# One run of twelve matmuls for a head's value product, in place of six steps

## The chip, the cores and the metric

The kernel runs on one NeuronCore of a Trainium2 chip. The metric is the device time of one execution in microseconds (us), the median of several runs. TensorE (PE) does matmuls, and its weight loads are shown apart as PEld. VectorE is DVE, ScalarE is ACT, GpSimd is POOL, and SyncE (SP) issues the DMAs. Each engine has its own instruction stream. Where one needs another's result, it waits on a semaphore.

## The reference

Two layers follow each other. Attention comes first, with 4 batches, 8 heads, a sequence of 768 and a head size of 64. Keys outside a query's hash bucket are masked out.

```python
mask = q_bucket[:, :, :, None] == k_bucket[:, :, None, :]
scores = np.where(mask, scale * np.matmul(q, k.transpose(0, 1, 3, 2)), -1000000000.0)
attn = np.exp(scores - np.max(scores, axis=-1, keepdims=True))
attn = attn / (np.sum(attn, axis=-1, keepdims=True) + 1e-09)
attn_out = np.matmul(attn, v)
```

Then, with x of [4, 768, 512] put together from the 8 heads, a gated feed-forward layer with a causal convolution of width 5:

```python
gate = 1 / (1 + np.exp(-sum(conv_w[k] * xp[:, k:k + S, :] for k in range(5))))
out = (gate * (x @ w_val)) @ w_out
```

All is float32 (the feed-forward weights are float64 and are turned into float32 pairs in the kernel).

## The kernel before, in words

A unit is one head of one batch (32 units). A unit has six tiles of 128 queries, so there are 192 tiles. The main loop has one **slot** k per tile, 196 in all, and the order in which the loop's body issues instructions is the order in which each engine takes them (a manual schedule). Nothing reorders them later.

In slot k the loop issues, for each engine:

- ACT: two copies `pt` of the transposed weights of tile k-4 out of PSUM (`keep_transposed`), then the exponential `p` of tile k.
- DVE: the row maximum `nm` of tile k, the factor `gs`, the shift `nb` (and, in even slots, row sums and reciprocals of two tiles), then what the side work asks for.
- POOL: the normalising of tile k-2, and subtractions of the side work.
- PE: the scores `s` of tile k+1 (four matmuls, tiles `ak`,`aq` and `bk`,`bq`), then the side work's matmuls, then six transposes `tp` of tile k-3.

The scores have two PSUM buffers, so the scores of tile k+2 can be issued only when the exponential of tile k has read its buffer. The transposes have two buffers `tp`. The value product has one, `av`, and the feed-forward sums have one, `m`, while the loop runs.

The side work is cut into steps by Python generators. A list holds the generators of one kind, and `step` advances the first of them to its next `yield`:

- `avs` (`attn_v`): the value product of a unit. It is entered at the sixth tile's copy, which is in slot k with k % 6 == 3. Six steps, one for each block of 128 keys, two matmuls each (two halves of 384 queries, placed in the two column halves of the array). After the last step, ACT copies the result into `x`.
- `convs` (`pair_x`): for two heads together, the split of `x` in two parts (`xh` on DVE, `xl` on POOL), an empty step, five convolution steps of 768 columns on DVE, and after a batch's fourth pair the sigmoids on ACT.
- `moes` (`moe`): the feed-forward of a batch. A value chunk (`val`, called V below) has three steps of four matmuls. After the third, DVE multiplies with the gate (`ht`), and at the next step's end casts the product (`hh`), from which POOL subtracts (`hl`). An output chunk (`outp`, called O below) has three steps of four matmuls with 512 columns and then a copy out of PSUM, on ACT or, near the sigmoids, on DVE. The last two output chunks of a batch are held back until the next batch's feed-forward has been entered.
- `weights`: loading and converting the feed-forward weights, on all engines but PE.
- `preps`: a unit's operands (cast `aq` on DVE in a slot with k % 6 == 5, subtraction `bq` on POOL and DMAs in the next), and every fourth unit the hash bits (`u` on DVE after 8 small matmuls).

After the loop come what is left of `avs`, the last convolutions and sigmoids, and the last batch's feed-forward.

## Time and profile before

| | |
|---|---|
| median of 3 runs | 646.72 us (646.63 to 647.21) |
| the profiled execution, its span from first to last instruction | 645.6 us |
| what lies outside of the span, against the median | 1.1 us |
| PE busy | 610.7 us, 95% of the span |
| DVE busy | 489.4 us, 76% |
| ACT busy | 424.5 us, 66% |
| POOL busy | 355.5 us, 55% |
| granted TensorE clock | 0.991 mean |

The span counts from the first to the last instruction of one profiled execution. Shares are averages over stages which differ: weights are converted in the first quarter, the feed-forward works beside the attention later, and it is alone at the end. A matmul in float32 is two PE instructions. In rows of the timeline the first number is the start in us from the span's start, and the second is the time from the start of the first to the end of the last instruction merged into the row. PE's instructions overlap, so what one costs is the distance between starts.

### The profile page before, as it was taken

What the parts mean: (1) busy time and instruction counts of PE and PEld (TensorE: products, weight loads), DVE (VectorE), ACT (ScalarE), POOL (GpSimd) and SP (SyncE); (2) the same over time, 40 slices, a digit from 0 to 9 for tenths busy, and PEclk for the clock granted to TensorE, in tenths of its full rate; (3) what the DMA queues carried; (4) which work ended last, traced back from release to release, by engine and by line L of the source; (5) the groups of instructions that cost most, each with busy time, mean ns of one, the idle gap of its engine ahead of it and who ended that gap; (6) DMA issues with size and microseconds to landing.
All of it is one profiled execution on the core that took longest, in us unless ns stands there. A gap on an engine that the chain in (4) does not pass through costs nothing.

```text
span 645.6 us, 10637 instructions
## 1 busy us (share of the span) xinstructions
PE 610.7 (95%) x3496; PEld 412.7 (64%) x3496; DVE 489.4 (76%) x1064; ACT 424.5 (66%) x881; POOL 355.5 (55%) x326
## 2 busy tenths in 40 slices
PE   4799998988999999999999999999999999999997
PEld 2565554555557666676667776676657777666895
DVE  5788999999996876769785887658695787656532
ACT  3487776767778666667878676576788666665300
POOL 1375868577765663566653656456563566536221
PEclk9799999999999999999999999999999999999999
DMA  6533435343432324233333234243332313300111
GB/s 239 126 100 78 137 102 136 110 123 89 104 78 66 81 66 133 70 103 95 103 79 104 59 79 118 71 117 79 99 75 60 79 30 79 84 18 1 49 50 49
DMA packets 23269, 56.76 MB, mean 88 GB/s; under 512 B 4296, under 2 KB 4296, under 8 KB 23216
## 3 DMA queue, kind: packets, MB, share of 16 engines
q1 hardware_dynamic: 23072, 56.06, 32.2%
q8 instruction: 28, 0.46, 0.3%
q14 instruction: 25, 0.20, 0.1%
q10 hardware_dynamic: 144, 0.03, 0.0%
HBM read 23.12 MB, written 6.29 MB: 46 GB/s over the span
## 4 chain that ended last, share of the span: by engine, by line
PE 70%; DVE 20%; ACT 5%; DMA 2%; issue 2%; POOL 0%; SPq 0%; DVEq 0%; ACTq 0%
PE av L303 17%; PE s L232 16%; PE tp L280 16%; PE m L390 8%; PE m L365 7%; DVE nm L238 7%; DVE nb L248 3%; ACT p L256 2%; DVE g L334 2%; DVE w L100 1%; PE tp L365 1%; PE tp L390 1%; PE s L390 1%; DVE gs L244 1%; PE tp L194 1%
## 5 line engine op out<-in xcount | busy, mean ns | idle before, releaser
L271 POOL TENSOR_SCALAR p<-p,ri 128x768 f32<-128x768 f32 x192 | 211.8, 1108 | 212.6 <-DVE nb L248 142.6
L289 ACT COPY pt<-tp 128x384 f32<-128x384 f32 x384 | 165.2, 481 | 100.9 <-PE tp L280 99.4
L256 ACT ACTIVATE p<-s,nb,gs 128x768 f32<-128x768 f32 x192 | 191.9, 1000 | 56.4 <-DVE nb L248 51.4
L238 DVE TENSOR_REDUCE nm<-s 128x1 f32<-128x768 f32 x192 | 182.5, 951 | 48.3 <-PE s L232 47.7
L280 PEld LDWEIGHTS tp<-ident,p 128*128 128x128 f32 x1152 | 125.4, 142 | 112.5 <-issue 75.4
L280 PE MATMUL tp<-ident,p 128*128 128x128 f32 x1152 | 169.4, 284 | 0.8 <-ACT pt L289 0.4
L303 PE MATMUL av<-pt,vt 128*64 128x384 f32 x768 | 168.7, 511 | 0.3 <-ACT x L311 0.3
L232 PE MATMUL s<-ak,aq 76*128 76x384 f32 x384 | 118.0, 388 | 24.9 <-ACT p L256 20.3
L232 PE MATMUL s<-bk,bq 128*128 128x384 f32 x384 | 102.2, 348 | 0.0
L232 PEld LDWEIGHTS s<-ak,aq 76*128 76x128 f32 x384 | 59.5, 195 | 36.9 <-ACT p L256 29.2
L303 PEld LDWEIGHTS av<-pt,vt 128*64 128x64 f32 x768 | 41.3, 135 | 58.8 <-issue 51.3
L248 DVE TENSOR_TENSOR nb<-nm,gs 128x1 f32<-128x1 f32 x192 | 73.8, 384 | 3.6 <-DVE ri L266 0.2
L334 DVE SCALAR_TENSOR_TENSOR g<-x,cw_sb,g 128x768 f32<-128x768 f32 x64 | 72.9, 1139 | 0.2
L232 PEld LDWEIGHTS s<-bk,bq 128*128 128x128 f32 x384 | 72.0, 194 | 0.4 <-issue 0.4
L168 POOL TENSOR_TENSOR bq<-r,aq 128x768 fp32r<-128x768 f32 x31 | 58.3, 1882 | 0.5 <-DVE aq L166 0.5
L376 POOL TENSOR_TENSOR hl<-ht,hh 128x384 fp32r<-128x384 f32 x32 | 32.8, 1026 | 32.3 <-DVE hh L374 32.3
L324 POOL TENSOR_TENSOR xl<-x,xh 128x384 fp32r<-128x384 f32 x32 | 33.2, 1050 | 29.6 <-DVE xh L323 29.6
L365 PE MATMUL m<-xh,wv 128*128 128x384 f32 x200 | 42.6, 337 | 0.0
L311 ACT COPY x<-av 64x384 f32<-64x384 f32 x64 | 30.3, 473 | 17.9 <-PE av L303 17.0
L370 DVE TENSOR_TENSOR ht<-m,g 128x384 f32<-128x384 f32 x25 | 13.9, 557 | 32.8 <-PE m L365 29.1
L256 ACT ACTIVATION_READ_ACCUMULATOR p<-s,nb,gs 128x1 f32 x192 | 38.6, 201 | 0.0
L390 PE MATMUL m<-wo,hh 128*128 128x512 f32 x144 | 38.2, 395 | 0.0
(84 smaller groups left out, 471.5 us busy)
## 6 DMA issues: line engine op xcount, KB each, us to landing
r<-in_qk_dram SPq DMA_DIRECT2D x32, 384.0 KB
vt<-in_v_dram SPq DMA_DIRECT2D x16, 384.0 KB
out_dram<-o SPq DMA_DIRECT2D x24, 256.0 KB
ak<-aq SPq DMA_DIRECT2D x31, 192.0 KB
bk<-aq SPq DMA_DIRECT2D x31, 192.0 KB
bk<-bq SPq DMA_DIRECT2D x31, 192.0 KB
bq<-aq SPq DMA_DIRECT2D x31, 192.0 KB
w<-in_w_val_dram SPq DMA_DIRECT2D x4, 512.0 KB
```

What stands on the lines that cost most here:

```text
L168: nc.gpsimd.tensor_tensor(out=bq, in0=r, in1=aq.bitcast(FP32), op=ALU.subtract)
L232: nc.tensor.matmul(out=s[:, hf, 0:HS], lhsT=lq[0:n, qs], rhs=rk[0:n, hf * HS:(hf + 1) * HS], start=n == M, stop=n == P)
L238: nc.vector.tensor_reduce(out=nm, in_=s[:, :, 0:HS], axis=AX.XY, op=ALU.max, negate=True)
L248: nc.vector.tensor_tensor(out=nbs[k], in0=nms.pop(k), in1=gs[k], op=ALU.mult)
L256: nc.scalar.activation(out=p, in_=s[:, :, 0:HS], func=AF.Exp, bias=nb, scale=gs.pop(k), accum_out=sm[:, k % 2:k % 2 + 1])
L271: nc.gpsimd.tensor_scalar(out=p, in0=p, scalar1=rcs.pop(k), scalar2=1.0, op0=ALU.mult, op1=ALU.mult)
L280: nc.tensor.transpose(out=tp[:, n * P:(n + 1) * P], in_=p[:, kb * P:(kb + 1) * P], identity=ident)
L289: nc.scalar.copy(out=pt[:, :, qo:qo + P], in_=tp[:, 0:HS].rearrange("p (a b) -> p a b", b=P))
L303: nc.tensor.matmul(out=av[s * D:(s + 1) * D, 0:HS], lhsT=vt[:, kb, hh * D:(hh + 1) * D], rhs=pt[kb // 3][:, kb % 3, :], start=(kb == 0), s ...
L334: nc.vector.scalar_tensor_tensor(out=g, in0=x[:, k:k + S], scalar=w, in1=g, op0=ALU.mult, op1=ALU.add)
L365: nc.tensor.matmul(out=acc[:, 0:HS], lhsT=wv[wi][:, c, j * P:(j + 1) * P], rhs=xs_[(c, o)][xi], start=(m == 0), stop=(m == 11))
L390: nc.tensor.matmul(out=acc, lhsT=hs[(o, j)][hi][:, tb * P:(tb + 1) * P], rhs=wo[wi][:, j, :], start=(m == 0), stop=(m == 11))
```

## The change

In the slot in which a unit's value product is entered (k % 6 == 3), all six steps are now done, one run of 12 matmuls and the copies into `x`. That slot does no feed-forward step and up to four convolution steps. Of the other five slots, odd ones do a convolution step (all of them after a batch's last pair, and in the last ten slots) and each does one feed-forward step, the one with k % 6 == 1 two. Slots after the sigmoids still do three. Comments have been taken out as well.

```diff
@@ attn_v
         if hh == 1:
             if c == 0:
                 cur["xs"], cur["g"] = {}, []
+            cur["last"] = c == NP - 1
             convs.append(pair_x(b, c, x, cur["g"], cur["xs"]))
...
-    cur["gates"], cur["end"], cur["pts"] = 0, False, []
+    cur["gates"], cur["end"], cur["pts"], cur["last"] = 0, False, [], False
...
             if k < N:
                 exponentials(k)
-            if k >= 60 or k % 2:
+            whole = bool(avs)
+            for _ in range(4 if whole else 1 if k % 2 or k >= N - 10 or cur["last"] else 0):
                 step(convs)
             for _ in range((1, 0, 2, 0, 2, 2)[k % 6]):
                 step(weights[turn])
                 turn = 1 - turn
-            for _ in range(3 if cur["gates"] else 1):
+            for _ in range(0 if whole else 3 if cur["gates"] else 1 + (k % 6 == 1)):
                 step(moes)
             cur["gates"] = max(0, cur["gates"] - 1)
             step(preps)
-            step(avs)
+            finish(avs)
             if 0 <= k - LAG < N:
                 transposes(k - LAG)
```

What this makes of the order is shown for slots 117 to 121, a stretch with six value steps to a unit. First PE in slots 117 and 118, before:

```order
L232 MATMUL s<-ak,aq 128x384 x2
L232 MATMUL s<-bk,bq 128x384 x2
L365 MATMUL m<-xh,wv_118 128x384 x4
L303 MATMUL av<-pt,vt 64x384 x2
L280 MATMUL tp<-ident,p 128x128 x6
L232 MATMUL s<-ak,aq 128x384 x2
L232 MATMUL s<-bk,bq 128x384 x2
L365 MATMUL m<-xh,wv_119 128x384 x4
L303 MATMUL av<-pt,vt 64x384 x2
L280 MATMUL tp<-ident,p 128x128 x6
```

PE in the same two slots, now (117 is a slot with k % 6 == 3):

```order
L232 MATMUL s<-ak,aq 128x384 x2
L232 MATMUL s<-bk,bq 128x384 x2
L303 MATMUL av<-pt,vt 64x384 x12
L280 MATMUL tp<-ident,p 128x128 x6
L232 MATMUL s<-ak,aq 128x384 x2
L232 MATMUL s<-bk,bq 128x384 x2
L366 MATMUL m<-xl,wv_118 128x384 x4
L280 MATMUL tp<-ident,p 128x128 x6
```

All twelve `av` matmuls stand in slot 117 between the scores of tile 118 and the transposes of tile 114, the value step of that slot is gone, and slot 118 has no `av`. The chunk of value steps ends in 118 (its third group is the one with `xl`).

PE in slot 121, now:

```order
L232 MATMUL s<-ak,aq 128x384 x2
L232 MATMUL s<-bk,bq 128x384 x2
L366 MATMUL m<-xl,wv_118 128x384 x4
L366 MATMUL m<-xh,wv_118 128x384 x4
L280 MATMUL tp<-ident,p 128x128 x6
```

The slot with two feed-forward steps ends one chunk and begins the next, in the one buffer `m`.

DVE in slots 118 to 120 (after the four convolution steps of slot 117), now:

```order
L238 TENSOR_REDUCE nm<-s 128x1
L262 TENSOR_SCALAR s_4550<-sm 128x2
L244 TENSOR_SCALAR gs<-nm 128x1
L266 RECIPROCAL ri<-s_4550 128x2
L248 TENSOR_TENSOR nb<-nm,gs 128x1
L371 TENSOR_TENSOR ht<-m,g 128x384
L238 TENSOR_REDUCE nm<-s 128x1
L244 TENSOR_SCALAR gs<-nm 128x1
L248 TENSOR_TENSOR nb<-nm,gs 128x1
L335 SCALAR_TENSOR_TENSOR g<-x,cw_sb,g 128x768
L375 CAST hh<-ht 128x384
L166 CAST aq<-r 128x768
```

The product `ht` stands in slot 118 ahead of the maximum of tile 119, and a convolution step, `hh` and `aq` stand in slot 119 ahead of the maximum of tile 120. Before, the products stood in other slots (119 and 122 among them), beside convolution steps of single slots.

## The prediction

> **What bounds the kernel now.** I read busy time by stages first. The first row runs from the scores of tile 10 (just ahead of the first value step) to those of tile 58, the second from there to the end of the last value product. Columns: length; PE, PEld, DVE, ACT, POOL busy with their instructions; PE's clock; DMA.

> ```profile
> 38.09:174.42 136.33, 121.70 (x705) 72.04 (x705) 129.54 (x269) 99.52 (x214) 93.37 (x82) 1.00 0.40 109
> 174.42:599.38 424.96, 423.23 (x2492) 287.47 (x2489) 314.37 (x707) 301.13 (x625) 237.93 (x219) 1.00 0.30 78
> ```

> DVE sets the pace of the first stretch (129.5 of 136.3 us), PE of the second (423.2 of 425.0). The tail to 645.6 takes 46.3 us. The groups of costs on DVE (mean ns behind the comma):

> ```profile
> L248 DVE TENSOR_TENSOR nb<-nm,gs 128x1 f32<-128x1 f32 x192 | 73.8, 384 | 3.6 <-DVE ri L266 0.2
> L334 DVE SCALAR_TENSOR_TENSOR g<-x,cw_sb,g 128x768 f32<-128x768 f32 x64 | 72.9, 1139 | 0.2
> L166 DVE CAST aq<-r 128x768 fp32r<-128x768 f32 x31 | 18.5, 596 | 0.0
> L323 DVE CAST xh<-x 128x384 fp32r<-128x384 f32 x32 | 18.0, 585 | 8.2 <-ACT x L311 7.3
> L374 DVE CAST hh<-ht 128x384 fp32r<-128x384 f32 x32 | 16.2, 508 | 0.3
> ```

> **What PE saves.** The timeline of PE in a slot with a value step, in one without side work, and at the loop's end, where the last unit's 12 matmuls (24 instructions) already stand in a row:

> ```profile
> 217.44 0.59 PE L232 MATMUL s<-ak,aq 76*128 76x384 f32 x2
> 217.87 0.52 PE L232 MATMUL s<-bk,bq 128*128 128x384 f32 x2
> 218.23 0.86 PE L365 MATMUL m<-xh,wv 128*128 128x384 f32 x4
> 219.02 0.87 PE L303 MATMUL av<-pt,vt 128*64 128x384 f32 x4
> 219.81 0.87 PE L280 MATMUL tp<-ident,p 128*128 128x128 f32 x6
> 220.44 0.60 PE L232 MATMUL s<-ak,aq 76*128 76x384 f32 x2
> ...
> 34.23 0.52 PE L232 MATMUL s<-bk,bq 128*128 128x384 f32 x2
> 34.58 0.82 PE L280 MATMUL tp<-ident,p 128*128 128x128 f32 x6
> ...
> 594.86 4.59 PE L303 MATMUL av<-pt,vt 128*64 128x384 f32 x24 [0.25 <-ACT x L311]
> 599.38 1.90 PE L390 MATMUL m<-wo,hh 128*128 128x512 f32 x7
> ```

> The tail shows the feed-forward without interruption, a chunk of V, a chunk of O, and when DVE gets the product:

> ```profile
> 607.75 1.55 PE L365 MATMUL tp<-xh,wv 128*128 128x384 f32 x8
> 609.83 1.55 PE L365 MATMUL s<-xh,wv 128*128 128x384 f32 x8
> 610.10 0.56 DVE L370 TENSOR_TENSOR ht<-tp,g 128x384 f32<-128x384 f32 x1 [1.40 <-PE tp L365]
> 620.90 1.99 PE L390 MATMUL s<-wo,hh 128*128 128x512 f32 x8
> 623.65 1.99 PE L390 MATMUL m<-wo,hh 128*128 128x512 f32 x8
> ```

> From starts: scores 0.43 + 0.36 = 0.79; V 2.08 / 3 = 0.70 a step, O 2.75 / 3 = 0.92; a value product's step 0.80, with 0.09 more ahead of it (V to `av` 0.79, not 0.70) and 0.05 behind (transposes busy 0.87, not 0.82, so 0.58 instead of 0.63). Six steps cost 6 x 0.94 = 5.6, the run 4.52 + 0.14 = 4.7. PE is spared 1.0 us a unit. A slot is now 0.79 + 0.70 + 0.58 = 2.07 with a V, 2.29 with an O and 1.37 with neither, where it was 3.0, 3.2 and 2.3. Without other waits a unit with six V takes 6 x 2.07 + 4.7 = 17.1 (before 18.0).

> **What these short slots meet.** The scores of tile k+2 need the exponential of tile k. The links of this loop:

> ```profile
> 316.29 0.86 ACT L289 COPY pt<-tp 128x384 f32<-128x384 f32 x2 [0.47 <-PE tp L280]
> 316.33 0.59 PE L232 MATMUL s<-ak,aq 76*128 76x384 f32 x2
> 317.03 1.01 ACT L256 ACTIVATE p<-s,nb,gs 128x768 f32<-128x768 f32 x1
> 317.32 0.96 DVE L238 TENSOR_REDUCE nm<-s 128x1 f32<-128x768 f32 x1 [0.94 <-PE s L232]
> 318.50 0.16 DVE L248 TENSOR_TENSOR nb<-nm,gs 128x1 f32<-128x1 f32 x1
> ...
> 100.72 0.62 DVE L248 TENSOR_TENSOR nb<-nm,gs 128x1 f32<-128x1 f32 x1
> 101.43 0.99 ACT L256 ACTIVATE p<-s,nb,gs 128x768 f32<-128x768 f32 x1 [1.52 <-DVE nb L248]
> 102.56 0.62 PE L232 MATMUL s<-ak,aq 76*128 76x384 f32 x2 [0.77 <-ACT p L256]
> ...
> 599.48 0.97 ACT L311 COPY x<-av 64x384 f32<-64x384 f32 x2 [3.79 <-PE av L303]
> ```

> Scores to maximum 0.99; maximum to the end of `nb` 1.34; 0.1 to the exponential, 1.0 for it, 0.14 to the next scores: 3.6 for two slots. A slot of 3.0 had 2.4 to spare over two slots, now V slots have 0.5. DVE takes its instructions in order, so every operation of the side work between `nb` and the next maximum uses up that spare time.

> I follow one unit with six V (slot W is the one with the run, time 0 the start of its scores):

> - PE: scores 0.79, run from 0.88 to 5.40, transposes, scores of W+2 at 6.03, V of slot W+1 from 6.82 to 7.52.
> - ACT: exponential of W, then nothing until the run ends, since the copies of tile W-3 wait for transposes behind it. `x` 5.5 to 6.5, copies 0.74, exponential of W+1 at 7.2 to 8.2: scores of W+3 at 8.4, 0.3 after PE could.
> - DVE: idle after the maximum of W+1 and the convolutions (4 x about 1.1, under the run). `ht` of slot W+1 waits for that slot's V: 7.8 to 8.4 (0.56). The maximum of W+2, ready since 7.0, stands behind it: `nb` at 9.7. Then slot W+2's side work, convolution 1.14 (or twice `xh`, 1.17), `hh` 0.51, `aq` 0.60, together 2.25: 12.0. `nb` of W+3 at 13.3, its exponential 13.4 to 14.4, scores of W+5 at 14.6, where PE was ready at 13.1.
> - Slot W+4 has two V, and the second begins a chunk in the one buffer `m`, which `ht` must have read: 14.6 + 0.79 + 0.70 + 0.27 + 0.56 + 0.1 + 0.70 + 0.58 = 18.3. Slot W+5 adds 2.07: **20.4 us** to the next unit.

> PE is spared 1.0 and stalls 3.3. The shortest rows of these casts (0.36 for `hh`, 0.55 for `aq`) would make it 19.8; if only the waits for the exponential and for `m` held PE, 18.3.

> **The sum.** First stretch: DVE has the same work and 5.2 us more of it by tile 58 (three convolutions, a first one of 0.6, two `xh`), since the batch's last pair is now done two units earlier. In slots W that come without convolutions it also starves: it needs the scores of W+2, which now come 6.0 after those of W+1, and has about 3 us of work until then: 2.9 idle in up to five such units, less what the 6.8 already idle can take up. Bounds 5.2 and 19.7; I take 9: tile 58's scores at 183.4.

> Second stretch, 22 units to tile 190 by the order's content, each by the same steps:
> - eight with six V: 8 x 20.4 = 163.2;
> - three with a V and five O: the same to 14.6, then two O in one slot, the second waiting some 0.9 for ACT's copy out of `m`, and one more: 21.0 each, 63.0;
> - three with four O and two V, no `ht` in W+1: 8.4 + 2.3 + 2.3 + 3.95 + 2.05 = 19.0 each, 57.0;
> - two with a V and three O: 20.1 each, 40.2;
> - three without feed-forward: at least 8.4 + 2 x 3.6 = 15.6, with DVE's side work 16.2 to 17.6 (before 13.9): 51.4;
> - three which open a batch (7 or 8 steps of PE, 0.3, 0.9 and about 0.6 of waits): 63.5;
> - ten groups of small matmuls for hash bits at 0.7: 7.0.

> Together 445.3. From tile 190's scores to the last run 15 (a chain with few slots left to fill), the run 4.5, and a tail of 46.3 less three O steps now done before, 43.5. 183.4 + 445.3 + 15 + 4.5 + 43.5 = 691.7 for the span, and with the 1.1 between the span and the median **692 us**, 7% slower. POOL's work is the same and no DMA is added. On SP's queue the loads of values (`vt`) and the stores move up by up to seven places. The loads waited there for a buffer:

> ```profile
> SPq L153 <- PE av L303: 20.4, 13, 3.5
> ```

> That buffer now comes free with the run, two slots ahead of the load's own slot, so I cost this at nothing; were it late, a unit's copies behind it would be up to 3.5 later, in a unit that gives them five slots.

> POOL may add to this. The row of `nb` above has a mean of 0.38 where the free one took 0.16. [...] By that the two `nb` of the chain would cost 0.45 more in some 17 units, and the sum would be 700. I leave it out of the sum, since such a wait may fall where DVE idles.

> **Rivals.**

> *PE keeps the pace (faster).* If DVE and ACT made up in the run what they miss after it, 22 units of the second stretch would each be 1.0 shorter and the first stretch as long as now: 646.7 - 22 = 625. For it: PE is busy 423.2 of 425.0 there, while DVE has 110 us idle. Against: that idle time would now lie inside of the run, where its inputs are missing. [...]

> *The stalls stay small.* DVE does not hold PE, but after each run PE waits 0.3 for the exponential, in each slot with two steps 0.9 for `m`, and units without feed-forward follow ACT and the loop (2.3 more in three units). PE's own sum of the second stretch is 425 less 22, and 3 for the O steps out of the tail, 406; 22 x 0.3 + 14 x 0.9 + 7 = 26 more make 432, 7 above now; the first stretch is 5 longer, the tail 3 shorter: 646.7 + 7 + 5 - 3 = 656. For it: DVE has 26% free there. Against: the chain above has no free link.

> *Nothing changes.* What PE gains is lost again within 0.2%, about what a measurement of this kernel can tell from no change: 647.

> **How the numbers follow.** Forecast (692 and its neighbourhood, 670 to 710) 0.63, small stalls (650 to 670) 0.22, faster 0.10, nothing 0.04, more than 710 0.01. Slower by over 0.2% therefore 0.86, the same 0.04, faster 0.10. The forecast's own range: the unit of 19.8 and the lower bound of the first stretch give 692 - 17 x 0.6 - 4 = 678; the page's sum is 700, and the upper bound of the first stretch adds 10: 710. The range for 8 in 10 reaches down into the second case: 655 to 706.

> **What would show it.** PE's busy time falls to about 580 us in any case. If I am right, its idle time grows to about 110 us; the scores wait for ACT's `p`, above all those of slot W+4; DVE's longest waits are for `ht` and for the scores behind the run; ACT shows a gap of about 3.5 us in every run; units of six V last about 20 us. If such units last 17 to 17.5 us, the loop is not the limit and the first rival holds. If the runs take other than 4.5 us, or DVE reaches `ht` before slot W+1's V is done, the working is wrong at its root.

## The result and the profile after

The changed kernel takes **720.82 us** (median of 4 runs, 718.51 to 722.36) against 646.85 us (4 runs, 646.63 to 647.21): a ratio of 1.114, with an interval of 1.1119 to 1.116. It is slower, as forecast, but by 74 us where 45 were forecast, and the range of 655 to 706 does not hold the time.

The profiled execution has a span of 718.6 us. First its busy time by stages, with the forecast's borders: scores of tile 10 to scores of tile 58, from there to the scores of tile 190, and the rest. Columns: stretch, length, busy time of PE, PEld, DVE, ACT and POOL (instructions), PE's granted clock, DMA share, GB/s. After:

```profile
37.72:200.54 162.82, 132.19 (x704) 90.21 (x704) 127.19 (x273) 99.43 (x216) 93.05 (x83) 0.85 0.35 93
200.54:653.40 452.86, 405.22 (x2393) 303.89 (x2393) 307.27 (x685) 287.82 (x604) 212.63 (x212) 0.97 0.29 73
653.40:718.60 65.20, 58.83 (x303) 48.44 (x300) 24.61 (x46) 16.89 (x32) 15.91 (x17) 0.97 0.10 37
```

The kernel before, with the same borders:

```profile
38.09:174.39 136.30, 121.67 (x704) 72.01 (x705) 129.51 (x269) 99.49 (x214) 93.34 (x82) 1.00 0.40 109
174.39:579.07 404.68, 403.20 (x2375) 274.30 (x2374) 301.36 (x683) 290.68 (x603) 227.10 (x209) 1.00 0.32 82
```

Three things are to be seen. Both stretches are longer, the first by 26.5 us and the second by 48.2, with nearly the same instructions on every engine (PE is busy for longer in the first because its clock was lower, 0.85 for 1.00). In the first, DVE set the pace and was idle for 6.8 us; now it is idle for 162.8 - 127.2 = 35.6. In the second, PE was idle for 1.5 us and is now idle for 47.6. And the clock is no longer 1.00. The page's row of the clock over the 40 slices, and its shares of the chain that ended last, after:

```profile
PEclk9898788888989899998999999999999899999999
...
PE 58%; DVE 27%; ACT 9%; issue 4%; DMA 1%; DVEq 0%; ACTq 0%
```

In the chain of before PE had 70% and DVE 20%. What waits for what, in the first stretch, sum, number and longest, after:

```profile
PE s L232 <- ACT p L256: 28.4, 29, 2.5
...
DVE nm L238 <- PE s L232: 22.9, 14, 4.2
```

The same two waits, before:

```profile
PE s L232 <- ACT p L256: 13.9, 22, 1.4
...
DVE nm L238 <- PE s L232: 1.6, 4, 0.9
```

DVE now starves for scores behind the runs (22.9 us for 1.6), and PE then waits for the exponential that hangs on DVE. In the second stretch, after:

```profile
DVE ht L371 <- PE m L366: 46.7, 15, 6.6
...
DVE nm L238 <- PE s L232: 44.2, 34, 4.2
PE s L232 <- ACT p L256: 29.9, 30, 2.5
...
PE m L366 <- DVE ht L371: 6.1, 9, 0.7
PE m L391 <- ACT o L399: 4.2, 3, 1.4
PE m L366 <- ACT o L399: 4.1, 5, 1.1
```

Two of these rows before, where PE's waits for the exponential came to 1.2 us in this stretch and those for `m` to none:

```profile
DVE nm L238 <- PE s L232: 44.2, 46, 1.9
...
DVE ht L370 <- PE m L365: 25.8, 15, 2.3
```

These are the waits that the forecast named: `ht` and the scores behind the run on DVE, the exponential and the one buffer `m` on PE. DVE's total for the scores is the same 44.2 as before; what is new there is fewer and longer waits (4.2 for 1.9). The `ht` and PE's own waits grew.

One unit with six V steps shows the loop at its place. The timeline of PE, ACT, DVE and POOL from the scores of tile 118, which open the slot with the run of unit 117 (after; rows left out):

```profile
411.18 0.60 PE L232 MATMUL s<-ak,aq 76*128 76x384 f32 x2
...
412.06 4.09 PE L303 MATMUL av<-pt,vt 128*64 128x384 f32 x24
...
416.08 0.88 PE L280 MATMUL tp<-ident,p 128*128 128x128 f32 x6
...
416.20 0.96 ACT L311 COPY x<-av 64x384 f32<-64x384 f32 x2 [3.22 <-PE av L303]
...
416.71 0.59 PE L232 MATMUL s<-ak,aq 76*128 76x384 f32 x2
...
418.47 0.56 DVE L371 TENSOR_TENSOR ht<-m,g 128x384 f32<-128x384 f32 x1 [2.00 <-POOL p L271]
...
418.95 0.94 DVE L238 TENSOR_REDUCE nm<-s 128x1 f32<-128x768 f32 x1
...
419.08 0.61 PE L232 MATMUL s<-ak,aq 76*128 76x384 f32 x2
...
421.50 0.62 PE L232 MATMUL s<-ak,aq 76*128 76x384 f32 x2
...
423.28 0.99 ACT L256 ACTIVATE p<-s,nb,gs 128x768 f32<-128x768 f32 x1 [1.09 <-DVE nb L248]
...
424.15 1.83 POOL L168 TENSOR_TENSOR bq<-r,aq 128x768 fp32r<-128x768 f32 x1
...
424.28 1.72 DVE L248 TENSOR_TENSOR nb<-nm,gs 128x1 f32<-128x1 f32 x1
...
424.42 0.62 PE L232 MATMUL s<-ak,aq 76*128 76x384 f32 x2 [0.60 <-ACT p L256]
...
426.81 0.96 PE L366 MATMUL m<-xh,wv 128*128 128x384 f32 x4 [0.72 <-DVE ht L371]
...
428.18 0.59 PE L232 MATMUL s<-ak,aq 76*128 76x384 f32 x2
...
430.23 0.59 PE L232 MATMUL s<-ak,aq 76*128 76x384 f32 x2
```

The run, 12 matmuls in 24 PE instructions (the rows of the scores and the transposes have one to a matmul), takes 416.08 - 412.06 = 4.02 us, ACT has a gap of 3.22 until it ends, `ht` stands ahead of the maximum at 418.95 (its row names POOL, but it also needs the V that starts at 417.51 and takes 0.86), the scores at 424.42 wait 0.60 for the exponential, and the second step of that slot waits 0.72 for `m`. The unit takes 430.23 - 411.18 = 19.05 us, where it took 18.04 before.

### The profile page after: what moved, and what is told of

Read it like the earlier page. It is cut to its first block, busy times and chain, and to the rows that moved or that the text cites. A ratio compares the mean times of both kernels' runs of the same rounds, so it can differ in the third digit from the quotient of the medians.

```text
span 718.6 us, 10628 instructions
## 1 busy us (share of the span) xinstructions
PE 618.4 (86%) x3496; PEld 457.7 (64%) x3496; DVE 485.8 (68%) x1061; ACT 421.3 (59%) x884; POOL 335.4 (47%) x326
## 4 chain that ended last, share of the span: by engine, by line
PE 58%; DVE 27%; ACT 9%; issue 4%; DMA 1%; DVEq 0%; ACTq 0%
PE av L303 18%; PE s L232 14%; PE tp L280 9%; DVE nm L238 9%; PE m L366 7%; PE m L391 5%; ACT p L256 4%; DVE nb L248 4%; DVE aq L166 3%; DVE ht L371 2%; DVE gs L244 1%; DVE hh L375 1%; PE tp L194 1%; PE s L391 1%; DVE g L335 1%
## 5 line engine op out<-in xcount | busy, mean ns | idle before, releaser
L271 POOL TENSOR_SCALAR p<-p,ri 128x768 f32<-128x768 f32 x192 | 185.2, 971 | 244.3 <-DVE nb L248 195.1
L256 ACT ACTIVATE p<-s,nb,gs 128x768 f32<-128x768 f32 x192 | 192.2, 1001 | 93.2 <-DVE nb L248 86.7
L238 DVE TENSOR_REDUCE nm<-s 128x1 f32<-128x768 f32 x192 | 182.4, 950 | 69.0 <-PE s L232 68.7
L289 ACT COPY pt<-tp 128x384 f32<-128x384 f32 x384 | 166.7, 485 | 58.3 <-PE tp L280 56.9
L232 PE MATMUL s<-ak,aq 76*128 76x384 f32 x384 | 126.7, 413 | 71.1 <-ACT p L256 63.9
L280 PE MATMUL tp<-ident,p 128*128 128x128 f32 x1152 | 170.8, 287 | 5.8 <-ACT pt L289 2.7
L280 PEld LDWEIGHTS tp<-ident,p 128*128 128x128 f32 x1152 | 142.0, 148 | 45.2 <-issue 23.6
L303 PE MATMUL av<-pt,vt 128*64 128x384 f32 x768 | 137.3, 507 | 0.0
L232 PEld LDWEIGHTS s<-ak,aq 76*128 76x128 f32 x384 | 63.5, 207 | 97.8 <-ACT p L256 89.0
L232 PE MATMUL s<-bk,bq 128*128 128x384 f32 x384 | 107.4, 363 | 0.2 <-issue 0.2
L303 PEld LDWEIGHTS av<-pt,vt 128*64 128x64 f32 x768 | 55.4, 142 | 72.1 <-issue 71.4
L311 ACT COPY x<-av 64x384 f32<-64x384 f32 x64 | 30.3, 473 | 105.1 <-PE av L303 104.6
L232 PEld LDWEIGHTS s<-bk,bq 128*128 128x128 f32 x384 | 77.2, 208 | 0.7 <-issue 0.7
L248 DVE TENSOR_TENSOR nb<-nm,gs 128x1 f32<-128x1 f32 x192 | 72.7, 378 | 3.4
L335 DVE SCALAR_TENSOR_TENSOR g<-x,cw_sb,g 128x768 f32<-128x768 f32 x64 | 66.1, 1033 | 1.4
L366 PE MATMUL m<-xh,wv 128*128 128x384 f32 x208 | 48.3, 358 | 10.1 <-DVE ht L371 6.1
L371 DVE TENSOR_TENSOR ht<-m,g 128x384 f32<-128x384 f32 x26 | 14.5, 557 | 56.9 <-PE m L366 52.5
L366 PEld LDWEIGHTS m<-xh,wv 128*128 128x128 f32 x208 | 38.2, 198 | 15.4 <-DVE ht L371 9.1
```

The lines of the kernel that those rows point to most:

```text
L232: nc.tensor.matmul(out=s[:, hf, 0:HS], lhsT=lq[0:n, qs], rhs=rk[0:n, hf * HS:(hf + 1) * HS], start=n == M, stop=n == P)
L238: nc.vector.tensor_reduce(out=nm, in_=s[:, :, 0:HS], axis=AX.XY, op=ALU.max, negate=True)
L248: nc.vector.tensor_tensor(out=nbs[k], in0=nms.pop(k), in1=gs[k], op=ALU.mult)
L256: nc.scalar.activation(out=p, in_=s[:, :, 0:HS], func=AF.Exp, bias=nb, scale=gs.pop(k), accum_out=sm[:, k % 2:k % 2 + 1])
L271: nc.gpsimd.tensor_scalar(out=p, in0=p, scalar1=rcs.pop(k), scalar2=1.0, op0=ALU.mult, op1=ALU.mult)
L280: nc.tensor.transpose(out=tp[:, n * P:(n + 1) * P], in_=p[:, kb * P:(kb + 1) * P], identity=ident)
```

## The experiments

The theory on record, A in short: short slots behind the run expose the loop of scores, maximum, shift and exponential (two slots long), and DVE starves behind a run; in the first stretch the clock falls as well, because PE waits. The rivals put the loss into one part alone: the run, the new places of the side steps, or the clock. Each edit is a diff against the kernel before or against the changed one, as its sentence says. Where three lengths are given, they are the first stretch, the second and the rest of the span (before: 136.3, 404.7, 66.6; changed: 162.8, 452.9, 65.3). Half clock is the time inside of the span with a granted clock under full (before 11.2 us, changed 88.7). Where no number of runs is given, a kernel ran once; the four runs of the changed kernel lie within 3.9 us of each other.

### The two halves of the change

**The run alone** (against before; all other steps stay where they were):

```diff
-            step(avs)
+            finish(avs)
```

> The kernel before with one edit: the value product is done in one run of 12 matmuls, while convolution and feed-forward steps stay where they were (one feed-forward step in every slot, the run's slot too; one convolution step in every odd slot and from slot 60 in every slot). Theory A (score loop and DVE's order: the five short slots cannot hide the chain scores, maximum, exponential, and DVE starves in the run): about as slow as the change, 705 to 740 us, and with no convolutions put under the run rather slower. Theory B (the new places of convolution and feed-forward steps are to blame, the run itself helps): 625 to 650 us. Theory C (the cost is TensorE's clock, granted at half after idle stretches): slow too, 690 to 730, with half-clock stretches around the runs.

Measured: 683.52 us; 162.4, 419.2 and 62.9. Half clock 59.7 us. That is slow, but below the range of theory A (705 to 740) and of the clock alone (690 to 730), and far above the range for the places alone. Its two stretches:

```profile
37.17:199.59 162.42, 133.40 (x704) 91.91 (x705) 122.72 (x270) 99.47 (x216) 94.48 (x84) 0.85 0.35 93
199.59:618.76 419.17, 391.37 (x2395) 295.86 (x2394) 300.10 (x690) 286.78 (x602) 234.62 (x210) 1.00 0.31 79
```

**The places alone** (against the changed kernel; the value product is again six steps, the convolution and feed-forward steps keep the new places):

```diff
-            whole = bool(avs)
+            whole = k >= 9 and k % 6 == 3
...
-            finish(avs)
+            step(avs)
```

> The change without the run: the value product stays in six steps, convolution and feed-forward steps at their new places (no feed-forward step in slots with k % 6 == 3 but up to four convolution steps, two feed-forward steps in slots with k % 6 == 1). Theory A: no DVE starvation, and slots of 2.3 to 3.7 us that hide most of the loop; what is left is the wait for the one buffer m in slots with two steps (0.9 in some 17 units) and four convolutions in a slot of 2.3 (about 1.6 in every second unit): 660 to 680 us. Theory B: most of the change's 74 us, 700 or more. Theory C: TensorE does not idle long enough, clock 0.99, near 650.

Measured: 668.15 us; 140.2, 422.4 and 66.5. Half clock 17.1 us.

```profile
37.27:177.51 140.24, 122.94 (x704) 73.56 (x705) 131.70 (x270) 100.19 (x214) 96.18 (x83) 0.98 0.40 106
177.51:599.86 422.35, 411.34 (x2387) 279.25 (x2386) 298.06 (x684) 289.61 (x602) 220.09 (x209) 1.00 0.31 79
```

What follows: the first stretch is lost to the run alone (26.1 us of 26.5, with or without the new places), and the low clock there comes with it. In the second stretch the halves cost 14.5 and 17.7 us, and together 48.2: they make each other worse by some 16 us. The run takes PE's work out of the slots that follow, and the new places put a second feed-forward step, with its wait for `m`, into one of them; how the 16 us divide between this and the clock is not shown by these two runs. Each alone has one low stretch of the clock there, of 3.4 us; together they have 30.5 us (0.97).

### The clock

**Filler matmuls** (against the changed kernel; in the slots 9 to 57 without a run, PE does six more 128x128 matmuls on a constant whose result nobody reads, so this kernel has work added):

```diff
+            if 9 <= k < 58 and not whole:
+                filler = ps_v.tile([P, 512], FP32, name="av")
+                for _ in range(6):
+                    nc.tensor.matmul(out=filler[:, 0:P], lhsT=ident, rhs=ident, start=True, stop=True)
```

> The change with six more matmuls (128x128, on the identity, result never read, about 1.3 us a slot) behind the transposes of every slot from 10 to 57 without a run: TensorE is kept busy where it waits for DVE. Theory C: the half-clock stretches between 50 and 200 us vanish, scores of tile 10 to tile 58 take 145 to 150 us instead of 162.8, and the span falls to about 702 to 706. Theory A without the clock (DVE's starvation in the run is all of the first stretch's loss): that stretch stays at 160 or gets longer by what the added matmuls cost, span 716 to 730.

Measured: 711.55 us; 161.4, 444.6 and 65.4. Half clock 13.7 us, none of it in the first stretch.

```profile
38.14:199.53 161.39, 158.94 (x1184) 130.17 (x1185) 130.85 (x276) 100.10 (x218) 96.11 (x85) 1.00 0.36 96
```

In the first stretch two things changed at once: the fillers brought the clock to 1.00, but PE is then busy for 158.9 of 161.4 us and sets the pace itself. It says nothing on what the clock costs there. The second stretch, which has no filler, was of use: it has 10.2 us at half clock instead of 30.5 (the low stretches at 200 and 241 us are gone), and is 8.3 us shorter.

**Half the fillers** (three instead of six):

```diff
-                for _ in range(6):
+                for _ in range(3):
```

> The change with three instead of six added matmuls a slot (slots 10 to 57 without a run, results never read): half the cover, about 0.6 us a slot, so that TensorE itself (159 of 161 us busy with six) does not set the pace. If half-clock stretches are part of the first stretch's loss: scores of tile 10 to tile 58 in 150 to 156 us instead of 162.8 (six matmuls: 161.4), span 702 to 708. If DVE's starvation alone makes it: 161 to 163 again.

Measured: 709.1 us; 154.5, 451.6 and 63.8.

```profile
37.34:191.88 154.54, 135.59 (x945) 104.05 (x945) 131.15 (x273) 98.36 (x216) 97.00 (x83) 1.00 0.37 98
```

Now neither PE (135.6) nor DVE (131.2) fills the 154.5 us, and the clock is 1.00. What follows: 8.3 us of the first stretch's loss were the clock, at least, since the filler itself may cost something. 18.2 us are left at full clock, and DVE's idle time accounts for them: 154.5 - 131.2 = 23.4 against 6.8 before is 16.6, and 1.6 more busy. In the second stretch the low clock fell into other units this time, so its length says little.

How the clock falls is seen in PE's rows (timeline of the changed kernel; slots before the run of slot 21, and the run):

```profile
68.28 0.82 PE L280 MATMUL tp<-ident,p 128*128 128x128 f32 x6
...
71.60 1.01 PE L232 MATMUL s<-ak,aq 76*128 76x384 f32 x2 [2.50 <-ACT p L256]
...
73.05 1.48 PE L280 MATMUL tp<-ident,p 128*128 128x128 f32 x6
...
79.07 4.93 PE L303 MATMUL av<-pt,vt 128*64 128x384 f32 x24
```

The stretches before, in and after it, columns as above:

```profile
60.00:70.60 10.60, 8.42 (x54) 5.61 (x50) 8.64 (x21) 5.41 (x13) 6.40 (x6) 1.00 0.19 51
70.60:80.80 10.20, 8.79 (x30) 6.81 (x32) 8.67 (x17) 6.55 (x14) 6.88 (x7) 0.50 0.60 157
80.80:94.50 13.70, 10.63 (x66) 7.01 (x62) 11.22 (x24) 7.96 (x18) 7.50 (x7) 1.00 0.28 74
```

A wait of 2.50 us, and in it the clock goes to 0.50 for 10.2 us. The same transposes then take 1.48 instead of 0.82, the run that falls into it 4.9 instead of 4.0, and the next scores come later: each such slot makes DVE starve longer (its idle time in the first stretch is 35.6 us here and 23.4 in the kernel with three fillers).

### The buffer `m` and the side work behind the run

**Two buffers** (against the changed kernel; in the slots with k % 6 of 4, 5 and 0, the feed-forward takes its sums in the idle bank of `av`):

```diff
+        if len(pools) == 1 and cur["k"] % 6 in (4, 5, 0):
+            return ps_v.tile([P, 512], FP32, name="av")
...
         for k in range(N + LAG + 1):
+            cur["k"] = k
```

> The change with a second accumulator for the feed-forward: chunks begun in slots with k % 6 in 4, 5, 0 use the bank of the value product, which is free between the runs, so that the second of two steps in a slot need not wait for the first chunk's reader. Theory A: 0.7 to 0.9 us less in some 14 units, part of it taken back where DVE comes next (units of six value steps gain 0.4 at most): span 706 to 713. Rival (DVE alone sets the pace): no change beyond 3 us.

Measured: 697.0 us; 161.0, 432.8 and 64.0. No wait for `m` is left; in the bank of `av` two of 2.0 us together come up. The waits for the exponential over the whole span, 63.9 us in the changed kernel, stay (sum, number, longest):

```profile
PE s L232 <- ACT p L256: 62.2, 69, 2.5
```

What follows: the direction is the theory's, the size is larger (23.5 us of the span). Units 117 and 165 with six V got 0.4 to 0.5 shorter, as the loop behind them left little to gain, but the units with five O steps 1.7 (69, 123 and 171: 20.43, 21.65, 21.65 to 18.74, 19.99, 20.00). Some 8 us of it stand in three units (57, 63, 159) which low stretches of the clock hit in the changed kernel, and here less or not at all. So the span gained more than the 14.4 us of waits for `m` (6.1 + 4.2 + 4.1); whether those waits are what brought the clock down in these units was not tried by itself.

**Five convolution steps under the run** instead of four (against the changed kernel), so that DVE has one less to do behind it:

```diff
-            for _ in range(4 if whole else 1 if k % 2 or k >= N - 10 or cur["last"] else 0):
+            for _ in range(5 if whole else 1 if k % 2 or k >= N - 10 or cur["last"] else 0):
```

> The change with five instead of four convolution steps in a run's slot, so that the fifth convolution no longer stands on DVE in the crowded slot W+2, but under the run. Theory A (the chain product, maximum, side work, maximum, exponential on DVE holds the scores of W+5): 0.8 to 1.0 us less in each of the nine units with k % 12 == 9 behind slot 57, and some in the first stretch: span 707 to 713. Rival (the loop without the side work, or TensorE, holds these units): no change.

Measured: 715.91 us; 161.8, 450.3 and 63.8: less than expected. The units which lost a convolution step behind `nb` did what the loop says: 117, 165, 141, 69 and 81 got 0.8 to 0.9 shorter (117 from 19.05 to 18.21). Of the nine that were to gain, 93, 129 and 177 did not change by more than 0.1 (the ninth, 189, has its slots in the tail). In the trace of the changed kernel, these three have no `ht` behind the `nb` of slot W+1, and the five that gained have one: the fifth convolution costs time only where `ht` has already put the loop back. And the low clock moved: 111 and 135, where there was none before, lost 1.3 and 2.8. The single step is shown; the sum mixes it with the clock.

**Run only from slot 57 on** (against the changed kernel; in the first stretch six steps, with the new places):

```diff
-            whole = bool(avs)
+            whole = k >= 9 and k % 6 == 3
...
-            finish(avs)
+            if k >= 57:
+                finish(avs)
+            else:
+                step(avs)
```

> The change with the value product back in six steps up to slot 56, the run of 12 from slot 57; all else as in the change. If the first stretch's loss comes from the run's starving of DVE and from the half-clock it brings: scores of tile 10 to tile 58 in 138 to 142 us (162.8 in the change, 140.2 with the new places alone), the second stretch unchanged at 445 to 453, span 692 to 700. If the new places of the convolutions are to blame there: 150 or more.

Measured: 682.25 us; 140.3, 439.0 and 63.8. The first stretch is that of the places alone, as expected. The second is shorter than expected: units 117 to 183 are as in the changed kernel (19.05, 21.68 and so on) but for 135, 153 and 159, which low stretches hit in one of the two kernels or in both, and the five units from 63 to 87 take 90.9 us and not 107.3. The first batch's last pair of heads becomes ready at another slot there, so that unit 57 holds six V and not eight, and in the units behind it a chunk of V ends in another slot. Units 63 and 81 show what that is worth, since they have the same steps in both kernels (six V, the run, the hash bits). In the changed kernel a chunk ends in W+1 and in W+4, here in W+3 and W+5, so that `ht` no longer stands in the slot behind the run, and the two V of W+4 belong to one chunk. Two rows of unit 81, which has its run from 256.79 on (`ht` of W+3, and W+4's V steps without a wait between them):

```profile
267.59 0.56 DVE L371 TENSOR_TENSOR ht<-m,g 128x384 f32<-128x384 f32 x1 [1.15 <-PE m L366]
...
268.75 1.55 PE L366 MATMUL m<-xh,wv 128*128 128x384 f32 x8
```

Unit 81 takes 18.36 us for 20.44, and unit 63 takes 18.14 where it took 21.07 without a low clock (in the kernel with three fillers). Both are below the 18.83 of unit 87 in the kernel before, which also has six V and hash bits. So it is not the run of 12 by itself that costs time in such a unit, but the run with `ht` in the slot behind it and a chunk's change in W+4.

### Runs in between: pairs and threes

If a run of 12 is too long for the loop and six single steps leave little for PE, two or three steps together may do. **Pairs** in odd slots from slot 57 on (against before):

```diff
-            step(avs)
+            for _ in range((2 if k % 2 else 0) if k >= 57 else 1):
+                step(avs)
```

> The kernel before with one edit: from slot 57 the value product's six steps are done two at a time in odd slots, none in even ones (three visits of the tiling mode a unit instead of six). Theory A: two neighbouring slots take 2 x 2.07 + 1.29 + 0.14 = 5.6 us, more than the loop's 3.6 and than the 5.0 with a product ht in it, so nothing stalls and three visits of 0.14 less in 22 units give 636 to 640 us. Rival: every slot without a value product's step loses as in the change, 650 or more.

Measured: **641.46 us** (4 runs, 640.85 to 641.87), a ratio of 0.9909 (0.9892 to 0.9925): 0.9% faster than the kernel before, a little above the expected range. 136.0, 399.8 and 65.7; its second stretch:

```profile
173.75:573.57 399.82, 390.73 (x2380) 284.84 (x2378) 293.47 (x686) 288.87 (x604) 234.95 (x210) 1.00 0.33 83
```

Its waits for the exponential there (sum, number, longest; 1.2 us in the kernel before):

```profile
PE s L232 <- ACT p L256: 5.7, 16, 1.1
```

PE has 12.5 us less to do than before (390.7 for 403.2) and gives back 7.6 of it in new idle time. A pair takes 1.44 us from start to start (its timeline of PE, 442.29 to 443.73):

```profile
442.29 1.51 PE L303 MATMUL av<-pt,vt 128*64 128x384 f32 x8
443.73 0.88 PE L280 MATMUL tp<-ident,p 128*128 128x128 f32 x6
```

**Threes**, in slots with k % 3 == 0:

```diff
-            step(avs)
+            for _ in range((3 if k % 3 == 0 else 0) if k >= 57 else 1):
+                step(avs)
```

> The kernel before with one edit: from slot 57 the six steps of a value product are done three at a time, in slots with k % 6 == 3 and k % 6 == 0. TensorE is spared four visits of 0.14 (the pairs three). Without stalls 632 to 636 us. Theory A: two short slots of 2.07 stand between the long ones, and a product ht there asks for 5.0 us, 0.8 more than they last, so that most of the gain is lost again: 640 to 648, not better than the pairs.

Measured: 645.49 us (10 runs), a ratio of 0.9974 (0.9964 to 0.9983). PE has the same 390.3 us of work in this second stretch, of 404.3 us: what is spared is nearly all given back.

**Pairs, with the convolutions as pairs in the same slots** (against before, beside the edit of the pairs):

```diff
-            if k >= 60 or k % 2:
+            for _ in range((2 if k % 2 else 0) if k >= 60 else k % 2):
                 step(convs)
```

> The kernel with pairs of value steps in odd slots from 57, and from slot 60 the convolution steps two at a time in odd slots, none in even ones, so that DVE's side work lies in the long slots. Theory A: what is left of waits for the exponential in the second stretch (5.7 us) falls to about 2: 636 to 640 us against 641.5. Rival (two convolutions in one slot crowd DVE as much): no gain, 641 to 644.

Measured: 648.49 us (10 runs), a ratio of 1.0022 (1.0012 to 1.0032): the hope that convolutions are best put beside the long slots fell, and the time is above the rival's range too. Two convolutions stand behind one `nb` and ahead of the next maximum: unit 117 takes 18.93 us for 17.54 with the pairs alone. The scores of one slot, with the pairs alone:

```profile
373.07 0.61 PE L232 MATMUL s<-ak,aq 76*128 76x384 f32 x2 [0.15 <-ACT p L256]
```

and with the convolutions as pairs:

```profile
377.09 0.62 PE L232 MATMUL s<-ak,aq 76*128 76x384 f32 x2 [0.80 <-ACT p L256]
```

**Threes, with the convolutions as threes in the same slots** (against before, beside the edit of the threes):

```diff
-            if k >= 60 or k % 2:
+            for _ in range((3 if k % 3 == 0 else 0) if k >= 60 else k % 2):
                 step(convs)
```

> The kernel with three value steps in slots with k % 3 == 0 from 57, and from slot 60 the convolution steps three at a time in those slots, none in the short ones. Theory A: the stalls of the threes come from side work of DVE in short slots; half of it is now under the long slots: 638 to 643 us against 645.5. Rival (the product ht alone holds the loop): 644 to 646.

Measured: 667.24 us (4 runs), a ratio of 1.0301 (1.0277 to 1.0325), a miss again and a larger one. The waits for the exponential over the span:

```profile
PE s L232 <- ACT p L256: 44.0, 53, 2.6
```

Some 40% of them stand ahead of a single position, the tiles with k % 12 == 3. The second stretch also has 20.5 us at half clock here, and none in the threes alone, so part of the loss is the clock's. So cover on PE does not help when it is in the slot in which DVE is filled up too: what has to be spread is DVE's side work between `nb` and the next maximum.

## Why the prediction was right and where it failed

The forecast's sum against the profiled execution's span, term by term:

| term | forecast | measured |
|---|---|---|
| scores of tile 58 at | 183.4 | 200.5 |
| tile 58 to tile 190 | 445.3 | 452.9 |
| tile 190 to the end (15 + 4.5 + 43.5) | 63.0 | 65.2 |
| span | 691.7 | 718.6 |

Of the 26.9 us that are missing, 17.1 are in the first term.

**The step that failed: "I take 9" for the first stretch**, between bounds of 5.2 and 19.7. It measured 26.5, outside of both. Two things were wrong in it.

- The starving of DVE was mis-sized. I had counted 2.9 us "in up to five such units, less what the 6.8 already idle can take up", and by taking 9 left 3.8 us for it beside 5.2 of added work. At full clock the half-strength fillers left 18.2, near the upper bound, and 16.6 of it are idle time of DVE: 14.7 more than before in the five units whose run comes without convolutions (slots 9, 15, 27, 39 and 51; about the full five times 2.9) and 1.9 in the other three (counted in the traces). So the old idle time took up nothing of it. The added operations came as counted (14 and 4 convolution steps for 11 and 3, eight `xh` for six), but DVE's busy time rose by 1.6 us there and fell by 2.3 in the changed kernel, in part because the `nb` took 17.4 and 18.7 us for 24.7. In the changed kernel, with its low clock, DVE idles for 3.0 to 6.5 us in every one of the eight units.
- The clock. The forecast held PE at the 1.00 of the first row of before in every term, and no rival had another. The low stretches cost 8 us or more here, and the term was put at nothing.

The forecast gave 0.01 to more than 710 us, where the result lies.

**The second stretch came within 7.6 us of its sum (452.9 for 445.3), and its mechanism was seen.** With 10.2 us at half clock instead of 30.5, the kernel with six fillers took 444.6 there. Low stretches cost about 3 us in a unit that they hit: unit 63 takes 23.83 us with one, 21.07 without. The single units were off on both sides. In the unit shown, with time 0 at the scores of tile 118:

| link | forecast | measured |
|---|---|---|
| length of the run | 4.52 | 4.02 |
| scores of W+2 | 6.03 | 5.53 |
| scores of W+3 | 8.4 | 7.90 |
| scores of W+5 | 14.6 | 13.24 |
| behind the slot with two V | 18.3 | 17.00 |
| next unit | 20.4 | 19.05 |

The run was taken from the loop's end, where it took half a microsecond longer. Runs of other than 4.5 us were one of the forecast's signs of being wrong at the root; here the 0.5 moved all that follows by as much, and the order of the links stayed. Most of the rest of the difference is DVE's side work, for which I took mean durations (2.25) and not the short ones that come here (420.19 to 421.86, 1.7). With the short casts I had named 19.8, and less the run's 0.5 that gives 19.3. Against that, units with five O steps took 20.4 to 21.7 (forecast 21.0), those with four O and two V 18.6 and 19.0 (forecast 19.0, units 177 and 75), the one with a V and three O that no low clock hit 18.7 (forecast 20.1, unit 141), those without feed-forward 16.9 to 18.0 (16.2 to 17.6), and units that open a batch 23 to 24 (21.2). So terms that were too long made up for terms that were too short and for the low clock: that the sum came so near is in part luck.

**The tail** was forecast at 63.0. It took 65.2 with a low stretch of the clock in it (3.4 us at 664.5) and 62.9 to 64.0 in the five kernels with a run that had none at that place.

**What would show it.** The waits for the exponential ahead of slot W+4's scores, the waits for `m`, DVE's for `ht` and the scores behind the run, and ACT's gap (3.22 in the unit shown) came as described. PE's busy time did not fall to 580 but rose to 618.4, since matmuls at half clock are busy for nearly twice as long (1.48 for 0.82 in the rows above); an estimate takes half of PE's busy time in the low stretches, 78.5 of their 88.7 us, off and comes to 579. Idle time was 100 us (forecast 110).

**The rivals.** PE keeps the pace (625): against it, the loop behind the run was the limit. The saving itself is there (a run of 4.02 and 0.14 beside it for six steps of 0.94, 5.6), but as PE's own time, and of the kernels with steps in a row only the pairs kept more than 0.5 us of it in the second stretch (4.9). The rows of before have 0.09 us ahead of a step and 0.05 behind it; the result shows that sparing them was not what decides. Small stalls (656): the kernel with the places alone (668) and the run alone (684) each lie above it. The shift `nb` waiting for POOL (700): the row at 424.28 is such a wait, 1.72 us long beside POOL's 1.83 from 424.15, and both end at 426.0. In the trace of the changed kernel 45 of the 192 `nb` took over 0.25 us, 0.30 to 1.77, and each of them ended within 0.03 us of the end of an instruction of POOL, as did 71 in the kernel before (counted in the traces); a median `nb` took 0.16. The wait at 424.28 cost PE nothing: the exponential behind it was done at 427.08, and the scores at 428.18 were held by `m`, whose reader `ht`, next on DVE, waited for its sums until 426.20 in any case. The 0.45 a unit behind the 700 of the forecast's range is an estimate from the rows of before, 2 x (0.38 - 0.16); no run shows it as a cost, and the groups of `nb` have nearly the same mean as before (0.384):

```profile
L248 DVE TENSOR_TENSOR nb<-nm,gs 128x1 f32<-128x1 f32 x192 | 72.7, 378 | 3.4
```

Which unit a low stretch of the clock falls into was not tried by itself (the last section has what the traces show of it): small edits (five convolutions, fillers in other units) moved them, and with them up to 3 us a unit, so differences of less than some 5 us between two such kernels say little.

## What to carry to other kernels

PE's time that is spared by putting one product in a row is only gained if the loop that feeds PE has room in every slot: put the length of that loop against the length of two slots before and after, slot by slot, and count DVE's in-order work between its links. What stands in the slot right behind a run matters most: units with the same steps took 2 to 3 us less where `ht` came two slots later. Do the same for the engine that sets the pace of each stretch: a long run on another engine starved it here (14.7 us more idle time in five units of the kernel with three fillers), and the 6.8 us that it was idle before took up none of that. Two steps in a row, in every second slot, kept part of the gain (0.9909), where a run of six lost 11%.

## What the runs showed of the hardware that was not expected

In the changed kernel the clock fell on waits shorter than its own stretches. The low stretches last 3.4, 6.8 or 10.2 us, at a granted clock of 0.50, and the longest single wait of PE for the exponential in the changed kernel is 2.6 us; the one quoted above begins in a wait of 2.50. Three 128x128 matmuls more in a slot were enough to keep the clock at 1.00 through the first stretch. Ahead of the low stretches PE was only partly idle.

And the low clock feeds on DVE's starving: a matmul at half clock brings the next scores later (six transposes took 1.48 us for 0.82), and DVE's maximum and the exponential come later. In the first stretch DVE is idle for 35.6 us in the changed kernel and for 23.4 in the one with three fillers, whose clock is 1.00 there. That this in turn brings the next low stretch is argued and not shown. The run alone had 59.7 us of half clock, the places alone 17.1, both together 88.7.
